# Three moves at the head of an attention-plus-MLP kernel: batch 0's sums inverted on ScalarE, batch 2 turned by DMA with its squares on VectorE, batch 1's last quad prepared earlier

## The chip, the cores and the metric

The kernel runs on one core of a Trainium2 chip. The metric is the device time of one execution in microseconds (us), as the median of several; lower is better. The core's engines each run their instructions in order: TensorE (PE in the profile; its weight loads are PEld), VectorE (DVE), ScalarE (ACT), GpSimd (POOL) and the queue of SyncE (SP), which here issues DMA transposes and output writes. SBUF and PSUM are memories of the core; in this kernel TensorE writes its results to PSUM. The span is the length of the one execution that was profiled.

## The reference

The inputs are q, k, v of shape (8 batches, 12 heads, 448 positions, 64) in float32 and two weights, 768x2048 and 2048x768.

```python
q_n = q / (norm(q, axis=-1) + 1e-6); k_n = k / (norm(k, axis=-1) + 1e-6)
scores = q_n @ k_n.T / tau                 # tau = 0.1
attn = softmax(scores)                     # the row sum divides
x = (attn @ v), heads side by side         # (3584, 768)
h = x @ w_in;  g = max(0.01 * h, h);  out = g @ w_out
```

## The kernel before

Each batch has six head pairs with two halves, so twelve *visits*. At a visit TensorE makes the scores of one half, ScalarE their exponentials. One visit later come parts of `weigh`: the row sums and the weighted values of a *quad* (four heads, two pairs). Layers 1 and 2 of the MLP for earlier tokens fill TensorE's time between visits. Meanwhile the q and k of the next batch are prepared: squares, their sums (`reduce`), the root (ScalarE), the inverse (VectorE), the multiply (`apply`), and the turn (transpose) so that the head dimension lies on partitions.

```python
def turn(b, what):                           # whole tensor, by DMA; batches 3 to 7
    xn, xt = st[what + "n", b], turned(b, what)
    nc.sync.dma_start_transpose(out=xt[...], in_=xn[...])

def turn_pair(b, p, eng=None):               # one pair, by TensorE; batches 0 to 2
    ...                                      # 8 transposes into a PSUM tile "mm"
    for i, what in enumerate("qk"):
        nc.vector.tensor_copy(out=turned(b, what)[...], in_=tp[:, i]...)

def inverse(b, g, sm, c0=0, c1=S):
    st["rs", b, g] = wk.tile([128, S], F32, name="rs")
    nc.vector.reciprocal(st["rs", b, g][:, c0:c1], sm[:, c0:c1])
    ...
def weigh(b, g, s, c0=0, c1=S):
    if s == 0:
        inverse(b, g, sums(b, g, c0, c1), c0, c1)   # sums: PSUM tile "pv", 2 buffers
    x_write(b, g, s, values(b, g, s, None, c0, c1), c0, c1)   # values: also "pv"
```

The two `pv` buffers matter: `values(b, g, 1)` takes the buffer that the sums of the same quad held, so TensorE can't start it before the inversion has read them. What is prepared for batches 1 and 2 during batches 0 and 1 stands in `early(b, n)`, n being the visit; its part for b == 1 is in the diff below. The order of issue in the program is the order of execution on each engine. (In the profiles Lnnn is a line of the kernel shown, so the same statement has other numbers in other kernels.) From batch 2 on, a general schedule is used:

```python
def after_scores(b, n):
    if b < 2:
        return early(b, n)
    if b + 2 < B and n < 2:
        load(b + 2, "qk"[n])                 # issued by GpSimd
    ...
    if n == 2:
        load(b + 1, "v")
        norm_sums(b + 1, "q")                # squares and reduce, both VectorE
```

Of the kernel before, what the change touches and what calls it, by code (L numbers as in the profile page):

```python
# [10 lines left out]
ACTF = mybir.ActivationFunctionType  # L11
# [5 lines left out]
def kernel(  # L17
# [18 lines left out]
    nc = tc.nc  # L36
# [4 lines left out]
    PK = S // NT  # L41
# [39 lines left out]
    st = {}  # L81


    def load(b, what, g0=0, g1=G):
        src = {"q": q_r, "k": k_r, "v": v_r}[what]
        if (what, b) not in st:
            if what == "v":
                st[what, b] = vpool.tile([PK, H, NT, D], BF16, name="v_bf")
            else:
                st[what, b] = bfpool.tile([PK, H, NT, D], BF16, name="qk_bf")  # L90
        if g1 - g0 == G:
            nc.gpsimd.dma_start(out=st[what, b], in_=src[b])  # L92
            return
        for g in range(g0, g1):
            nc.gpsimd.dma_start(out=st[what, b][:, g::G], in_=src[b][:, g::G])
# [19 lines left out]
    def norm_squares(b, what, eng, g0=0, g1=G):  # L115
        if (what + "n", b) not in st:
            st[what + "n", b] = inp.tile([PK, G, 2, NT, 2, D], BF16, name=f"{what}_n")
            st[what + "i", b] = small.tile([PK, G, 4, NT], F32, name=f"{what}_ni")
        for g in range(g0, g1):
            x, sq = by_quad(st[what, b])[:, g], squares(b, what, g, g + 1)[:, 0]  # L120
            if eng is nc.scalar:
                nc.scalar.activation(sq, x, func=ACTF.Square)
            else:
                eng.tensor_mul(sq, x, x)  # L124

    def norm_reduce(b, what, g0=0, g1=G):
        nc.vector.tensor_reduce(  # L127
            st[what + "i", b][:, g0:g1].rearrange("p g a t -> p (g a) t"),
            squares(b, what, g0, g1).rearrange("p g a t d -> p (g a) t d"),
            axis=AX.X, op=ALU.add,  # L130
        )

    def norm_sums(b, what, g0=0, g1=G):
        norm_squares(b, what, nc.vector, g0, g1)
        norm_reduce(b, what, g0, g1)

    def norm_root(b, what, g0=0, g1=G):
        ni = st[what + "i", b][:, g0:g1]
        nc.scalar.activation(ni, ni, func=ACTF.Ln, bias=tiny[:PK])
        nc.scalar.activation(ni, ni, func=ACTF.Exp, scale=0.5)  # L140

    def norm_inverse(b, what, g0=0, g1=G):
        ni = st[what + "i", b][:, g0:g1]
        nc.vector.tensor_scalar_add(ni, ni, 1e-6)
        nc.vector.reciprocal(ni, ni)  # L145

    def norm_apply(b, what, eng, g0=0, g1=G):
        x, xn, ni = by_quad(st[what, b]), st[what + "n", b], st[what + "i", b]
        for g in range(g0, g1):
            for j in range(2):  # L150
                ni_j = ni[:, g, 2 * j : 2 * j + 2]
                eng.tensor_tensor(  # L152
                    out=xn[:, g, j].rearrange("p t h d -> p h t d"),
                    in0=x[:, g, 2 * j : 2 * j + 2],
                    in1=ni_j.unsqueeze(3).to_broadcast([PK, 2, NT, D]),
                    op=ALU.mult,
                )


    def turned(b, what):  # L160
        if (what + "T", b) not in st:
            xt = tpool.tile([128, NT * HP * PK + 16], BF16, name=f"{what}T")
            nc.gpsimd.memset(xt[:, NT * HP * PK :], 0.0)
            st[what + "T", b] = xt
        return st[what + "T", b]

    def turn(b, what):
        xn, xt = st[what + "n", b], turned(b, what)
        nc.sync.dma_start_transpose(
            out=xt[:, : NT * HP * PK].rearrange("p (c n) -> p c n", n=PK),  # L170
            in_=xn.rearrange("p g j t h d -> p (g j t h d)"),
        )
# [21 lines left out]
    def scores(b, p, half, hold=False):  # L194

        qT, kT = st["qT", b], st["kT", b]
        if half == 0:
            st["pe", b, p] = epool.tile([PK, NT, 2, S], BF16, name="pe")
        wide = 128 if b > 2 else PK
        for i in range(2):  # L200
            ki = 2 * half + i
            sc = psc.tile([128, 2, 512], F32, name="sc")
            o = p * S + ki * PK
            for a in range(2):
                r = slice(64 * a, 64 * a + 64)
                nc.tensor.matmul(  # L206
                    out=sc[:wide, a, :S], lhsT=kT[r, o : o + wide],
                    rhs=qT[r, p * S : (p + 1) * S], start=True, stop=True,
                )
            st["exp", i] = (st["pe", b, p][:, ki], sc[:PK, :, :S])  # L210
            if i == 0 or not hold:
                exponential(i)
# [19 lines left out]
    def exponential(i):  # L232
        pe, sc = st["exp", i]
        nc.scalar.activation(out=pe, in_=sc, func=ACTF.Exp, scale=inv_tau)  # L234
# [10 lines left out]
    def x_place(b):  # L245


        if b % 2 == 0:
            st["x", b] = xpool.tile([128, KT, 512], BF16, name="xT")
            st["x64", b] = cpool.tile([128, KT, 64], BF16, name="x64")  # L250
        else:
            st["x", b] = xpool.tile([128, KT, 512], BF16, name="xT")
            nc.gpsimd.tensor_copy(out=st["x", b][:, :, 0:64], in_=st["x64", b - 1])

    def sums(b, g, c0=0, c1=S):
        sm = ppv.tile([128, S], F32, name="pv")
        columns(sm, b, g, lambda a, ki: ones[:PK, :], c0, c1)
        return sm

    def inverse(b, g, sm, c0=0, c1=S):  # L260
        st["rs", b, g] = wk.tile([128, S], F32, name="rs")
        nc.vector.reciprocal(st["rs", b, g][:, c0:c1], sm[:, c0:c1])  # L262
        if ("x", b) not in st:
            x_place(b)

# [96 lines left out]
    V, P, A = nc.vector, nc.gpsimd, nc.scalar  # L362
# [45 lines left out]
    sm = sums(0, 0, *one)  # L408
# [22 lines left out]
    sm = sums(0, 1, *one)  # L431
# [9 lines left out]
    sm = sums(0, 2, *one)  # L441
# [11 lines left out]
    def step(b, what, g0, g1, *steps):  # L453

        for name, eng in steps:
            if name == "squares":
                norm_squares(b, what, eng, g0, g1)
            elif name == "reduce":
                norm_reduce(b, what, g0, g1)
            elif name == "root":  # L460
                norm_root(b, what, g0, g1)
            else:
                norm_inverse(b, what, g0, g1)
                norm_apply(b, what, eng, g0, g1)

    def early(b, n):
        def both(to, g0, g1, name, eq=None, ek=None):
            step(to, "q", g0, g1, (name, eq))
            step(to, "k", g0, g1, (name, ek))

        if b == 0:
            if n == 0:
                both(1, 0, 1, "squares", P, P)
            elif n == 2:
                both(1, 0, 1, "reduce")
            elif n == 3:
                both(1, 1, 2, "squares", P, P)
            elif n == 4:
                both(1, 0, 1, "root")
            elif n == 5:  # L480
                both(1, 0, 1, "apply", V, P)
            elif n == 6:
                both(1, 1, 2, "reduce")
            elif n == 8:
                both(1, 1, 2, "root")
                both(1, 2, 3, "squares", P, P)
                load(2, "q")
            elif n == 9:
                both(1, 1, 2, "apply", V, P)
                load(2, "k")  # L490
            elif n == 11:
                both(1, 2, 3, "reduce")
        elif n == 1:
            both(1, 2, 3, "root")
            load(2, "v")
        elif n == 2:
            both(1, 2, 3, "apply", V, P)
        elif n == 4:
            step(2, "q", 0, 3, ("squares", P))
            load(3, "q")  # L500
        elif n == 5:
            step(2, "k", 0, 3, ("squares", P))
            load(3, "k")
        elif n == 6:
            step(2, "q", 0, 3, ("reduce", V))
        elif n == 7:
            step(2, "k", 0, 3, ("reduce", V))
            step(2, "q", 0, 3, ("root", A))
        elif n == 8:
            step(2, "q", 0, 3, ("apply", P))  # L510
            step(2, "k", 0, 3, ("root", A))
        elif n == 9:
            step(2, "k", 0, 3, ("apply", V))

    def after_scores(b, n):
        if b < 2:
# [22 lines left out]
            turn(b + 1, "k")  # L539

    turns = {
        (0, 7): (1, 0), (0, 8): (1, 1), (0, 10): (1, 2), (0, 11): (1, 3), (1, 3): (1, 4, 5),
        (1, 10): (2, 0, 1), (1, 11): (2, 2, 3), (2, 1): (2, 4, 5),
    }

    def after_dense(b, n):
# [15 lines left out]
    for b in range(B):  # L562
        for p in range(HP):
            for half in range(2):
                n = 2 * p + half
# [56 lines left out]
```

## Time and profile before

| | before |
|---|---|
| median | 481.35 us (479.99 to 481.79, 3 runs) |
| profiled span | 479.3 us |
| PE busy | 435.0 us, 91% |
| first scores of batch 2 (timeline of PE) | 107.52 us |
| longest wait of PE after the start | 4.66 us, until 102.20 |

The head of the profile page of the kernel before: busy time of each engine, then PE's busy tenths and its granted clock in 40 slices of 12 us.

```profile
PE 435.0 (91%) x3618; PEld 221.4 (46%) x3632; DVE 220.8 (46%) x267; ACT 269.3 (56%) x445; POOL 137.6 (29%) x152
...
PE   0788888758899999989899999998999999999996
...
PEclk9999999988999999998999999999999999999999
```

From slice 12 on, counted from 0 (144 us), PE is busy nearly all the time. What can be won lies before. The next lines are from the timeline of PE of the kernel before: start in us, duration in us, engine, source line, operation, output and inputs with shapes, count, and in brackets the idle time just ahead and what ended it.

```profile
96.95 0.59 PE L206 MATMUL sc<-qT,kT 64*112 64x448 bf16 x4
102.20 4.27 PE L319 MATMUL mm<-w_out_sb,hT 128*128 128x384 bf16 x16 [4.66 <-DVE kT L188]
...
107.52 0.59 PE L206 MATMUL sc<-qT,kT 64*112 64x448 bf16 x4
...
112.04 1.67 PE L239 MATMUL pv<-pe,v_bf 112*32 112x448 bf16 x16 [1.79 <-DVE rs L262]
```

At 102.20 PE had waited 4.66 us for the VectorE copy of kT: layer 2 needs a PSUM buffer that the turn of batch 2 holds until it is copied out. The timeline of VectorE of the kernel before shows why the copy was late:

```profile
88.14 2.95 DVE L262 RECIPROCAL rs<-pv 128x448 f32<-128x448 f32 x1
...
94.16 7.38 DVE L152 TENSOR_TENSOR k_n<-qk_bf,k_ni 112x512 bf16<-112x512 bf16 x6
101.47 0.38 DVE L188 COPY qT<-mm 128x448 bf16<-128x448 bf16 x1
```

Six multiplies of batch 2's k (94.16, 7.38 us) stood ahead of it. The same six operations, on GpSimd for q, ran at the same time. In windows of 2 us (busy time of PE, PEld, DVE, ACT, POOL with counts, then granted clock, DMA share, GB/s), the clock after the hole in the kernel before:

```profile
102.00:104.00 2.00, 1.80 (x6) 0.89 (x7) 0.74 (x3) 0.00 (x0) 0.77 (x1) 0.50 0.78 74
104.00:106.00 2.00, 2.00 (x10) 1.02 (x9) 0.00 (x0) 0.00 (x0) 0.00 (x0) 0.68 1.44 194
```

Granted clock 0.50 and 0.68: after the idle time TensorE ran at half speed, and the group of sixteen layer-2 matmuls took 4.27 us where others of the same kind took 2.77. The Trainium skill ("TensorE: Matmul & The Clock Gate", Part 1: The HAM clock gate) says that an idle window of about 3.4 us brings the array's clock to half. This hole agrees: 4.66 us idle, then clock 0.50.

### The profile page before, as it was taken

Reading aid. Unit: us, or ns where it says so; the run is one execution under the profiler, and the core shown is the slowest. Engines: PE = TensorE matmul, PEld = TensorE weight load, DVE = VectorE, ACT = ScalarE, POOL = GpSimd, SP = SyncE. Lnnn points to the kernel's source line nnn. Section 1 sums busy time; section 2 is a strip of 40 time slices with the busy share of each in tenths; the row PEclk is TensorE's granted clock in tenths of the full one; section 3 lists DMA queues with packets and bytes.
Section 4 is the critical chain, followed back from the end, with each engine's and each line's share of the span. In section 5 each row is a group of like instructions: output and inputs, shape, how many; then the busy total and the mean of one; then the engine's idle time right before and its main releaser. Section 6 shows DMA issues by size and latency. Waiting matters only on the chain.

```text
span 479.3 us, 8521 instructions
## 1 busy us (share of the span) xinstructions
PE 435.0 (91%) x3618; PEld 221.4 (46%) x3632; DVE 220.8 (46%) x267; ACT 269.3 (56%) x445; POOL 137.6 (29%) x152
## 2 busy tenths in 40 slices
PE   0788888758899999989899999998999999999996
PEld 0456644534344554544344554544434555454463
DVE  5976867865923087205923087208712312311000
ACT  3767567824675557653674557665774567543411
POOL 7555649450074012900073012700180000000000
PEclk9999999988999999998999999999999999999999
DMA  9999995557019860392419660455034110020022
GB/s 123 210 203 204 145 172 100 77 75 111 21 28 134 144 104 15 61 192 69 68 35 132 147 105 4 59 116 97 2 59 90 55 47 1 18 66 18 0 67 66
DMA packets 73924, 41.23 MB, mean 86 GB/s; under 512 B 29600, under 2 KB 73120, under 8 KB 73888
## 3 DMA queue, kind: packets, MB, share of 16 engines
q0 software_dynamic: 37728, 22.81, 34.5%
q1 hardware_dynamic: 36160, 17.90, 16.4%
q8 instruction: 28, 0.46, 0.4%
q14 instruction: 8, 0.07, 0.0%
HBM read 45.61 MB, written 11.01 MB: 118 GB/s over the span
## 4 chain that ended last, share of the span: by engine, by line
PE 76%; DVE 14%; DMA 3%; POOL 3%; ACT 2%; issue 1%; SPq 0%; POOLq 0%; ACTq 0%; DVEq 0%
PE mm L319 29%; PE mm L306 27%; PE pv L239 11%; PE sc L206 7%; DVE rs L262 3%; DVE k_ni L127 2%; DMA kT<-k_n 2%; DVE k_n L152 2%; DVE q_ni L127 2%; DVE q_n L152 2%; ACT pe L234 1%; POOL k_n L124 1%; POOL q_n L124 1%; PE sc L224 1%; PE mm L180 1%; DMA qk_bf<-in_q_dram 1%
## 5 line engine op out<-in xcount | busy, mean ns | idle before, releaser
L234 ACT ACTIVATE pe<-sc 112x896 bf16<-112x896 f32 (+2 forms) x192 | 167.9, 917 | 15.9 <-PE sc L224 10.2
L319 PE MATMUL mm<-w_out_sb,hT 128*128 128x384 bf16 x896 | 156.9, 332 | 4.7 <-DVE kT L188 4.7
L306 PE MATMUL mm<-xT,w_in_sb 128*128 128x512 bf16 (+3 forms) x850 | 155.1, 332 | 3.0 <-ACT hT L311 1.7
L262 DVE RECIPROCAL rs<-pv 128x448 f32<-128x448 f32 (+2 forms) x27 | 71.3, 2642 | 149.2 <-PE pv L239 149.2
L319 PEld LDWEIGHTS <-hT 128*128 128x128 bf16 x896 | 85.8, 99 | 74.7 <-issue 17.5
L306 PEld LDWEIGHTS <-w_in_sb 128*128 128x128 bf16 x864 | 76.5, 98 | 76.5 <-issue 18.1
L311 ACT ACTIVATE hT<-mm 128x512 bf16<-128x512 f32 (+3 forms) x144 | 71.8, 502 | 61.8 <-PE mm L306 61.2
L325 ACT COPY osb<-mm 128x384 f32<-128x384 f32 x56 | 26.8, 478 | 117.1 <-PE mm L319 84.3
L152 POOL TENSOR_TENSOR q_n<-qk_bf,q_ni 112x512 bf16<-112x512 bf16 x36 | 38.1, 1088 | 91.1 <-DVE q_ni L145 71.2
L206 PE MATMUL sc<-qT,kT 64*128 64x448 bf16 (+1 forms) x336 | 49.9, 360 | 8.2 <-ACT pe L234 6.0
L239 PE MATMUL pv<-pe,v_bf 112*32 112x448 bf16 (+2 forms) x864 | 48.1, 345 | 6.8 <-DVE rs L262 6.8
L152 POOL TENSOR_TENSOR k_n<-qk_bf,k_ni 112x512 bf16<-112x512 bf16 x40 | 41.8, 1071 | 7.8 <-DVE k_ni L145 4.7
L92 POOL DMA_DIRECT2D v_bf<-in_v_dram x8 | 7.5, 944 | 103.8 <-PE pv L239 103.7
L239 PEld LDWEIGHTS <-v_bf 112*32 112x32 bf16 x864 | 21.3, 99 | 26.4 <-issue 15.7
L206 PEld LDWEIGHTS <-kT 64*128 64x128 bf16 (+1 forms) x336 | 13.0, 103 | 38.5 <-issue 35.0
L127 DVE TENSOR_REDUCE k_ni<-k_n 112x16 f32<-112x1024 bf16 (+1 forms) x12 | 27.4, 2281 | 1.4 <-POOL k_n L124 1.2
L127 DVE TENSOR_REDUCE q_ni<-q_n 112x16 f32<-112x1024 bf16 (+1 forms) x12 | 27.3, 2277 | 0.2
L239 PE MATMUL pv<-pe,ones 112*32 112x448 bf16 (+2 forms) x432 | 24.5, 343 | 0.8 <-ACT pe L234 0.8
L278 DVE TENSOR_TENSOR xT<-pv,rs 128x448 bf16<-128x448 f32 x24 | 14.9, 622 | 20.4 <-PE pv L239 19.2
L281 DVE TENSOR_TENSOR xT<-pv,rs 128x384 bf16<-128x384 f32 (+2 forms) x30 | 14.3, 477 | 21.1 <-PE pv L239 19.5
L180 PE MATMUL mm<-ident,q_n 112*128 112x112 bf16 x72 | 7.7, 241 | 11.1 <-DVE q_n L152 10.5
L239 PEld LDWEIGHTS <-ones 112*32 112x32 bf16 x432 | 9.2, 97 | 13.1 <-issue 9.1
(48 smaller groups left out, 180.6 us busy)
## 6 DMA issues: line engine op xcount, KB each, us to landing
v_bf<-in_v_dram POOLq DMA_DIRECT2D x8, 672.0 KB, 7.5
qk_bf<-in_q_dram POOLq DMA_DIRECT2D x6, 672.0 KB, 7.4
qk_bf<-in_k_dram POOLq DMA_DIRECT2D x6, 672.0 KB, 9.4
w_in_sb<-in_moe_w_in_dram POOLq DMA_DIRECT2D x4, 768.0 KB, 19.1
w_out_sb<-in_moe_w_out_dram POOLq DMA_DIRECT2D x2, 1536.0 KB, 27.0
out_dram<-osb SPq DMA_DIRECT2D x16, 168.0 KB, 2.4
out_dram<-osb SPq DMA_DIRECT2D x16, 144.0 KB, 2.1
out_dram<-osb SPq DMA_DIRECT2D x16, 120.0 KB, 2.0
```

What stands on the lines that cost most here:

```text
L127: nc.vector.tensor_reduce(st[what + "i", b][:, g0:g1].rearrange("p g a t -> p (g a) t"), squares(b, what, g0, g1).rearrange("p g a t d -> ...
L152: eng.tensor_tensor(out=xn[:, g, j].rearrange("p t h d -> p h t d"), in0=x[:, g, 2 * j : 2 * j + 2], in1=ni_j.unsqueeze(3).to_broadcast([P ...
L206: nc.tensor.matmul(out=sc[:wide, a, :S], lhsT=kT[r, o : o + wide], rhs=qT[r, p * S : (p + 1) * S], start=True, stop=True,)
L234: nc.scalar.activation(out=pe, in_=sc, func=ACTF.Exp, scale=inv_tau)
L239: nc.tensor.matmul(out=dst[32 * a : 32 * a + 32, c0:c1], lhsT=weights(a, ki), rhs=st["pe", b, 2 * g + a // 2][:, ki, a % 2, c0:c1], start= ...
L262: nc.vector.reciprocal(st["rs", b, g][:, c0:c1], sm[:, c0:c1])
L278: nc.vector.tensor_mul(x[:, kt, 64:512], po, rs)
L281: nc.vector.tensor_mul(x[:, kt, c0:c], po[:, c0:c], rs[:, c0:c])
L306: nc.tensor.matmul(out=pm[:, :n], lhsT=w_in_sb[:, kt, m * 128 : (m + 1) * 128], rhs=st["x", b][:, kt, x0 : x0 + n], start=(kt == 0), stop= ...
L311: nc.scalar.activation(out=st["h", c][:, m, :n], in_=pm[:, :n], func=ACTF.Prelu, alpha=0.01)
L319: nc.tensor.matmul(out=po[:, :NH], lhsT=st["h", c][:, m, j0 : j0 + 128], rhs=w_out_sb[:, m, n * NH : (n + 1) * NH], start=(m == 0), stop=( ...
L325: nc.scalar.copy(out=osb, in_=po[:, :NH])
```

## The change

The intent can be read from the parts: take the slow VectorE reciprocals out of batch 0; take batch 2's transposes and their copies off TensorE and VectorE by using the DMA turn that later batches use; start batch 2's preparation earlier, for which batch 1's last quad must leave the shared buffers earlier.

```diff
-        wide = 128 if b > 2 else PK
+        wide = 128 if b > 1 else PK
@@ def inverse
-        nc.vector.reciprocal(st["rs", b, g][:, c0:c1], sm[:, c0:c1])
+        rs = st["rs", b, g][:, c0:c1]
+        if b == 0:
+            nc.scalar.activation(rs, sm[:, c0:c1], func=ACTF.Ln)
+            nc.scalar.activation(rs, rs, func=ACTF.Exp, scale=-1.0)
+        else:
+            nc.vector.reciprocal(rs, sm[:, c0:c1])
@@ def early, b == 1 (V, P, A: VectorE, GpSimd, ScalarE)
-        elif n == 1:
+        elif n == 0:
             both(1, 2, 3, "root")
             load(2, "v")
+        elif n == 1:
+            both(1, 2, 3, "apply", V, P)
+            load(3, "q")
         elif n == 2:
-            both(1, 2, 3, "apply", V, P)
-        elif n == 4:
-            step(2, "q", 0, 3, ("squares", P))
-            load(3, "q")
+            load(3, "k")
+        elif n == 3:
+            norm_sums(2, "q")
         elif n == 5:
-            step(2, "k", 0, 3, ("squares", P))
-            load(3, "k")
+            norm_sums(2, "k")
         elif n == 6:
-            step(2, "q", 0, 3, ("reduce", V))
+            step(2, "q", 0, 3, ("root", A), ("apply", P))
         elif n == 7:
-            step(2, "k", 0, 3, ("reduce", V))
-            step(2, "q", 0, 3, ("root", A))
-        elif n == 8:
-            step(2, "q", 0, 3, ("apply", P))
-            step(2, "k", 0, 3, ("root", A))
+            step(2, "k", 0, 3, ("root", A), ("apply", V))
         elif n == 9:
-            step(2, "k", 0, 3, ("apply", V))
+            turn(2, "k")
+            turn(2, "q")
@@ turns by TensorE
-        (0, 7): (1, 0), ..., (1, 3): (1, 4, 5),
-        (1, 10): (2, 0, 1), (1, 11): (2, 2, 3), (2, 1): (2, 4, 5),
+        (0, 7): (1, 0), ..., (1, 2): (1, 4, 5),
```

More of the change, by code (lines that the diff above doesn't have):

```diff
@@ L541 @@
     turns = {
-        (0, 7): (1, 0), (0, 8): (1, 1), (0, 10): (1, 2), (0, 11): (1, 3), (1, 3): (1, 4, 5),
-        (1, 10): (2, 0, 1), (1, 11): (2, 2, 3), (2, 1): (2, 4, 5),
+        (0, 7): (1, 0), (0, 8): (1, 1), (0, 10): (1, 2), (0, 11): (1, 3), (1, 2): (1, 4, 5),
     }
```

## The prediction

> **What bounds the kernel now.** TensorE: the page has PE busy 435.0 of 479.3 us (91%), the chain of waits is 76% PE. From 140 us on PE is near full (39.9 of 40 us between 340 and 420); only the first 132 us has anything to win. By the timeline of PE its waits there are: the start (12 us); in batch 0 the row-sum reciprocals (0.70 and 1.43 us of waiting in the first half, 1.35 at 65.0); in batch 1 one hole of 4.66 us (97.5 to 102.2), released by the VectorE copy of kT. That copy sits behind six VectorE multiplies of batch 2's k (94.16, 7.38 us; mean 1.23 beside GpSimd's multiplies against 0.65 alone). After the hole the granted clock is 0.50 and 0.68 for 4 us (windows of 2 us), and a 16-matmul group took 4.27 us against 2.77. The Trainium skill ("TensorE: Matmul & The Clock Gate", Part 1) says PE is throttled after an idle window of about 3.4 us; this hole agrees.
>
> **What the change does.**
> 1. Batch 0's six reciprocals (1.75 us for 256 columns, 1.35 for 192; 9.4 us of VectorE) become Ln and Exp on ScalarE, about 0.38 us each (estimate from the 128x256 Prelu, 0.38). PSUM is free after the Ln. Saved waits: 1 to 1.6 us by 36 us, 1.35 at 65. Part is lost at 59: the k multiplies on GpSimd wait for squares whose load ends at 53.2 anyway. Left: about 2 us.
> 2. Batch 2's six turn pairs leave PE: 0.95 us per two pairs and small gaps, 3 us in all, and 12 VectorE copies (3.6 us). They become two DMA transposes (3.2 to 8.2 us each in later batches).
> 3. Its squares go from GpSimd (11.3 us) to VectorE (3.6 us). The 4.66 us hole, as it stands, goes.
>
> **What it costs.** VectorE runs in order. norm_sums of q (5.2 us) now comes just before batch 1's first row-sum reciprocal, which should end near 79 instead of 77.9 us: about what was won so far is lost. Then ScalarE's root for k waits for the second reduce (near 86) and holds back activations: 1 to 2.5 us. Then the k multiply, 7.4 us beside GpSimd (the skill's "GPSIMD Engine Reference", section 1, says the two share SBUF interfaces; 1.23 against 0.65 agrees), stands before the second quad's reciprocal, at about 87 to 94. So I expect a new PE wait of 4 to 7 us at batch 1's tenth visit (values, near 91 to 97), again with a slow clock. The hole moves; it doesn't vanish. Turns end near 100 (k) and 104 (q), close to batch 2's first scores (before: 107.5); a wait there would be short.
>
> Sum: first scores of batch 2 about 1 to 3 us earlier, then 1.2 us from the removed last turns and 0.5 us from the full-width k weights; the PE-bound rest carries this shift to the end.
>
> **Prediction:** 477.5 us, 8 in 10 between 471 and 482. Faster by over 2%: 0.10; within 2%: 0.87; slower by over 2%: 0.03.
>
> **Right if** the profile shows: no PE wait for a kT copy near 100; a PE wait of several us on the batch-1 reciprocal behind the k multiplies, with low clock after it; PE's transposes 96 instead of 144; VectorE's row-sum reciprocals 21; PE from 140 on unchanged but shifted 2 to 5 us.
>
> **Wrong if** VectorE's k multiply runs near 0.65 us, so that the second hole is absent (then 8 to 10 us are won); if ScalarE, with the inversions in its queue, delays batch 0's exponentials and PE with them; or if the DMA turns land after batch 2's first scores are due.

## The result, and the profile after

The changed kernel takes 488.61 us (median of 4 runs, 488.38 to 489.77) against 481.09 (4 runs, 479.99 to 481.79): slower by 1.6%, ratio 1.0163 with a 95% interval of 1.0137 to 1.0189. Here and below a ratio is the mean time of one kernel's fast runs over that of the other's fast runs of the same rounds, so it isn't quite the ratio of the medians quoted.

| | before | after |
|---|---|---|
| profiled span | 479.3 | 487.8 us |
| PE busy | 435.0 | 435.2 us |
| first scores of batch 1 | 61.02 | 62.97 us |
| first scores of batch 2 | 107.52 | 116.62 us |
| from there to the end | 371.8 | 371.2 us |

The last two rows are sums of the rows above (span less the first scores). Batch 1's stretch grew from 46.50 to 53.65 us, by 7.15, while the start took 1.95 more and the rest 0.6 less; together that is the 8.5 us of the spans. (About 1.5 of the 1.95 us is a spell of slow clock from 50.8 to 54.2, which two other runs of the same instructions up to there did not have: see "Batch 0" below.) The page of the changed kernel, as before:

```profile
PE 435.2 (89%) x3570; PEld 219.6 (45%) x3584; DVE 214.7 (44%) x255; ACT 273.0 (56%) x457; POOL 127.1 (26%) x146
...
PE   0789887564899999997899999999899999999996
...
PEclk9999899967899999998999999999999999999999
```

Slices are 12.2 us here. Slices 7 to 9, counted from 0 (85 to 122 us), have fallen to 5, 6 and 4 tenths of PE. The timeline of PE of the changed kernel there:

```profile
92.17 0.59 PE L206 MATMUL sc<-qT,kT 64*112 64x448 bf16 x4
101.54 1.68 PE L239 MATMUL pv<-pe,v_bf 112*32 112x448 bf16 x16 [8.79 <-DVE rs L267]
103.16 2.10 PE L311 MATMUL mm<-xT,w_in_sb 128*128 128x128 bf16 x18
...
108.15 2.77 PE L324 MATMUL mm<-w_out_sb,hT 128*128 128x384 bf16 x16
116.62 0.93 PE L206 MATMUL sc<-qT,kT 64*128 64x448 bf16 x4 [5.70 <-DMA qT<-q_n]
...
122.23 1.69 PE L239 MATMUL pv<-pe,v_bf 112*32 112x448 bf16 x16 [0.71 <-DVE rs L267]
```

Where the kernel before waited once, the changed one waits twice: 8.79 us for the reciprocal, 5.70 us for the DMA turn of q. The first can be read on the timeline of VectorE of the changed kernel:

```profile
89.67 0.45 DVE L145 RECIPROCAL k_ni<-k_ni 112x48 f32<-112x48 f32 x1
90.16 8.47 DVE L152 TENSOR_TENSOR k_n<-qk_bf,k_ni 112x512 bf16<-112x512 bf16 x6
98.55 2.94 DVE L267 RECIPROCAL rs<-pv 128x448 f32<-128x448 f32 x1
```

The six k multiplies (now 8.47 us, 1.41 each) moved from visit 9 to visit 7, ahead of the second quad's reciprocal. By PE's timeline its sums were done at 89.04; it started at 98.55. For the second wait, first the timeline of GpSimd in the changed kernel:

```profile
89.79 8.29 POOL L152 TENSOR_TENSOR q_n<-qk_bf,q_ni 112x512 bf16<-112x512 bf16 x6 [16.62 <-PE pv L239]
...
98.37 0.98 POOL L92 DMA_DIRECT2D qk_bf<-in_q_dram  x1 [0.21 <-POOL kT L163]
99.35 0.94 POOL L92 DMA_DIRECT2D qk_bf<-in_k_dram  x1
```

and the timeline of SyncE's queue in the changed kernel:

```profile
98.78 7.08 SPq L169 DMA_TRANSPOSE kT<-k_n  x1
105.97 8.44 SPq L169 DMA_TRANSPOSE qT<-q_n  x1
```

The k turn is issued at 98.78, just after the k multiply. Almost at the same time (98.37 and 99.35) GpSimd issues the loads of batch 4's q and k: they belong to visits 0 and 1 of batch 2, but GpSimd has nothing else ahead of them and needs only the buffers of batch 2's q and k, which the multiplies have just freed. The transposes take 7.08 and 8.44 us, and PE starts 2.2 us after the second has ended (114.41). A turn of a later batch in the same run, without such company, takes 3.98 (149.05). The clock in windows of 2 us, changed kernel:

```profile
98.00:100.00 2.00, 0.00 (x0) 0.00 (x0) 2.00 (x2) 0.00 (x0) 1.79 (x5) 0.50 0.00 0
...
112.00:114.00 2.00, 0.00 (x0) 0.00 (x0) 0.00 (x0) 0.00 (x0) 0.00 (x0) 1.00 1.30 214
...
116.00:118.00 2.00, 1.38 (x12) 0.46 (x16) 0.00 (x0) 0.79 (x1) 0.00 (x0) 0.50 0.21 63
...
126.00:128.00 2.00, 2.00 (x14) 0.86 (x12) 1.97 (x2) 0.37 (x1) 0.00 (x0) 1.00 1.07 102
```

Besides the spell in batch 0, the clock is at half speed twice here: from 95 to 105 and from 116 to 126. An estimate of the cost, from group times at full and at half clock: the groups at 101.54 and 103.16 take 1.68 and 2.10 us against 0.94 and 1.37 in the kernel before, 1.5 us; the six groups from 116.62 to 123.84 lose another 4.0 against the same kinds later on. In the kernel before, three groups (4.27 for 2.77, 1.67 for 0.94, 3.68 for 2.77) lost 3.1.

### The profile page after: what moved, and what is told of

The parts are those of the page before. It is cut to its first block, busy times and chain, and to the rows that moved or that the text cites. A ratio compares the mean times of both kernels' runs of the same rounds, so it can differ in the third digit from the quotient of the medians.

```text
span 487.8 us, 8428 instructions
## 1 busy us (share of the span) xinstructions
PE 435.2 (89%) x3570; PEld 219.6 (45%) x3584; DVE 214.7 (44%) x255; ACT 273.0 (56%) x457; POOL 127.1 (26%) x146
## 4 chain that ended last, share of the span: by engine, by line
PE 75%; DMA 11%; DVE 7%; ACT 3%; SPq 2%; issue 1%; POOL 1%; POOLq 0%; ACTq 0%
PE mm L311 28%; PE mm L324 28%; PE pv L239 11%; PE sc L206 7%; DMA w_in_sb<-in_moe_w_in_dram 5%; DMA kT<-k_n 2%; DMA qT<-q_n 2%; DVE k_n L152 2%; ACT pe L234 2%; DMA qk_bf<-in_q_dram 1%; SPq L169 1%; DVE rs L267 1%; DVE q_n L152 1%; ACT hT L316 1%; DVE k_ni L127 1%
## 5 line engine op out<-in xcount | busy, mean ns | idle before, releaser
L324 PE MATMUL mm<-w_out_sb,hT 128*128 128x384 bf16 x896 | 154.3, 328 | 0.0
L267 DVE RECIPROCAL rs<-pv 128x448 f32<-128x448 f32 x21 | 62.1, 2955 | 157.4 <-PE pv L239 157.4
L311 PEld LDWEIGHTS <-w_in_sb 128*128 128x128 bf16 x864 | 77.6, 99 | 78.4 <-issue 19.8
L239 PE MATMUL pv<-pe,v_bf 112*32 112x448 bf16 (+2 forms) x864 | 50.0, 355 | 11.1 <-DVE rs L267 10.9
L239 PE MATMUL pv<-pe,ones 112*32 112x448 bf16 (+2 forms) x432 | 26.3, 364 | 1.1 <-ACT pe L234 1.1
L180 PE MATMUL mm<-ident,q_n 112*128 112x112 bf16 x48 | 5.6, 254 | 10.8 <-DVE q_n L152 10.5
```

Of the source, the lines that this page charges most:

```text
L239: nc.tensor.matmul(out=dst[32 * a : 32 * a + 32, c0:c1], lhsT=weights(a, ki), rhs=st["pe", b, 2 * g + a // 2][:, ki, a % 2, c0:c1], start= ...
L267: nc.vector.reciprocal(rs, sm[:, c0:c1])
L311: nc.tensor.matmul(out=pm[:, :n], lhsT=w_in_sb[:, kt, m * 128 : (m + 1) * 128], rhs=st["x", b][:, kt, x0 : x0 + n], start=(kt == 0), stop= ...
L324: nc.tensor.matmul(out=po[:, :NH], lhsT=st["h", c][:, m, j0 : j0 + 128], rhs=w_out_sb[:, m, n * NH : (n + 1) * NH], start=(m == 0), stop=( ...
```

## The experiments

The medians of the kernel before were 482.88, 481.63, 481.03 and 482.07 us on chips 8, 14, 2 and 14, so medians are compared only roughly; the ratios are safer. All kernels gave correct results.

### Late loads

The loads of batch 4 are put behind a load that has to wait, so that none runs during the two turns. Diff against the changed kernel:

```diff
-        if b + 2 < B and n < 2:
+        if b > 2 and b + 2 < B and n < 2:
             load(b + 2, "qk"[n])
@@
             load(b + 1, "v")
+            if b == 2:
+                load(4, "q")
+                load(4, "k")
```

> The changed kernel with batch 4's q and k loads issued behind batch 3's v load (which waits for a values group), so that no load runs during batch 2's two DMA transposes. Theory A (the transposes end late because the loads of batch 4 share the DMA with them): each transpose takes 3.2 to 4.5 us instead of 7.1 and 8.4, the 5.7 us wait of TensorE at batch 2's first scores shrinks to 0 to 1, the slow clock after it goes, and the time falls by 6 to 10 us to 479 to 483 us; the 8.8 us wait at the reciprocal stays. Rival B (transposes of this batch are slow in themselves, or only the late k multiply counts): time within 2 us of 488.6.

Measured: 482.33 us (4 runs), ratio to before 1.0025 (0.9974 to 1.0076), so 6.3 us below the changed kernel's median. The timeline of GpSimd with late loads:

```profile
115.56 0.98 POOL L92 DMA_DIRECT2D v_bf<-in_v_dram  x1 [18.93 <-PE pv L239]
116.53 0.94 POOL L92 DMA_DIRECT2D qk_bf<-in_q_dram  x1
```

and of SyncE's queue:

```profile
97.25 3.28 SPq L169 DMA_TRANSPOSE kT<-k_n  x1
100.64 3.38 SPq L169 DMA_TRANSPOSE qT<-q_n  x1
```

The transposes fell from 7.08 and 8.44 us to 3.28 and 3.38, and the wait of PE at batch 2's first scores (at 109.27) vanished, while the wait of 8.78 us for the reciprocal stayed. Theory A holds for the second wait: the turns were slow because of the loads beside them. (Not all slow clock after it went: PE waited 1.82 us for a reciprocal at 113.75, with a clock of 0.50 after.) The Trainium skill ("Trainium Kernel Development and Optimization", Key Constraints) says that DMAs of the Sync, Scalar and GpSimd queues all run on the same 16 engines and interleave. That agrees: 3.28 us alone, 7.08 in company.

### The k multiply behind the reciprocal

```diff
-            step(2, "k", 0, 3, ("root", A), ("apply", V))
+            step(2, "k", 0, 3, ("root", A))
+        elif n == 8:
+            step(2, "k", 0, 3, ("apply", V))
```

> The changed kernel with batch 2's k multiply one visit later, so behind the second quad's reciprocal in VectorE's order. Theory A (two waits in a row; the DMA transposes, which start only when the k multiply ends, set when batch 2 can start): the 8.8 us wait falls to under 2 us, but the k multiply ends 1 to 3 us later, the wait at batch 2's first scores grows from 5.7 to 11 to 16 us, time 487 to 491. Rival C (the reciprocal behind the k multiply is what costs): time falls by 6 to 9 us.

Measured: 485.64 us, ratio 1.0092 (1.0037 to 1.0146): about 3 us below the changed kernel, in neither theory's range. PE's timeline had no wait for the reciprocal over 1.5 us in batch 1, and one of 13.89 us for the q turn, as theory A said. The line of PE in this run:

```profile
112.80 0.93 PE L206 MATMUL sc<-qT,kT 64*128 64x448 bf16 x4 [13.89 <-DMA qT<-q_n]
```

What the theory had wrong is seen on VectorE's timeline:

```profile
87.48 2.90 DVE L267 RECIPROCAL rs<-pv 128x448 f32<-128x448 f32 x1
...
91.72 5.63 DVE L152 TENSOR_TENSOR k_n<-qk_bf,k_ni 112x512 bf16<-112x512 bf16 x6
```

The multiply started 3.1 us later than in the run with late loads (91.72 against 88.63) and still ended at nearly the same time (97.35 against 97.09): it took 5.63 us instead of 8.46, and GpSimd's multiplies of q ran beside it only until 95.0, which would explain it. In this run GpSimd's load of batch 4's k waited for VectorE's k multiply by the timeline of GpSimd:

```profile
97.65 0.94 POOL L92 DMA_DIRECT2D qk_bf<-in_k_dram  x1 [1.37 <-DVE k_n L152]
```

So the multiplies do release the loads; the turns, beside loads here too, took 6.37 and 6.58 us. Letting the reciprocal go first was free. Rival C falls all the same: a hole of 8.8 us was taken away and only about 3 us came of it (the interval overlaps that of the changed kernel), since batch 2 can't start before its turns have landed.

### Both moves

> Both moves at once. Theory A: first wait under 2 us, transposes 3.2 to 4.5 us each, wait at batch 2's first scores 5 to 9 us; time about that of the late loads alone, within 3 us, 478 to 483. Rival C: adds 6 to 9 us of gain to whatever the late loads alone give, so 471 to 475.

Measured: 479.53 us, ratio 0.9957 (0.9909 to 1.0004). The edit is the two diffs above together. PE's one long wait with both moves:

```profile
107.57 0.93 PE L206 MATMUL sc<-qT,kT 64*128 64x448 bf16 x4 [7.43 <-DMA qT<-q_n]
```

2.8 us below the late loads alone, in theory A's range. The first hole was taken away and became a wait for the q turn (7.43 us), in a chain of multiply, k turn, q turn. The loss of the changed kernel is now accounted for by the order of two pieces of work and the time of two loads; the three moves as such, so repaired, come to about the time of before.

### Batch 0's inversions back on VectorE

```diff
-        if b == 0:
+        if b < 0:
             nc.scalar.activation(rs, sm[:, c0:c1], func=ACTF.Ln)
```

> The changed kernel with batch 0's inversions back on VectorE. Theory D (moving them to ScalarE gave nothing, because in batch 0 TensorE then waited for w_in's load and for GpSimd's k multiplies, and VectorE's earlier multiply collided with GpSimd's squares): time within 2 us of the changed kernel, first scores of batch 1 at 61 to 63 us. Rival E (the inversions on ScalarE gave the 2 us that the prediction counted): 2 us or more slower than the changed kernel.

Measured: 488.18 us, ratio 1.0143 (1.0092 to 1.0195), against 1.0163 for the changed kernel: the same. First scores of batch 1 at 61.00 us. The inversions were worth nothing in this kernel.

### Batch 2 turned by TensorE again

```diff
-        wide = 128 if b > 1 else PK
+        wide = 128 if b > 2 else PK
@@ early
-            turn(2, "k")
-            turn(2, "q")
+            pass
@@ turns
+        (1, 10): (2, 0, 1), (1, 11): (2, 2, 3), (2, 1): (2, 4, 5),
```

> The changed kernel with batch 2 turned by TensorE as before the change; its early squares and multiplies on VectorE and the inversions on ScalarE stay. Theory A (the DMA turns cost a 5.7 us wait plus slow clock and save 3 us of TensorE): no wait for a DMA at batch 2's first scores, 8.8 us hole at the reciprocal stays, 482 to 486 us. Rival: the turns by DMA were a gain in themselves and the k multiply alone is to blame: 489 to 492.

Measured: 484.22 us, ratio 1.0055 (1.0023 to 1.0086), 4.4 us below the changed kernel; the wait of 8.78 us at the reciprocal stayed and there was no DMA wait at batch 2's first scores. As built, the DMA turns cost more than they saved; what is left of the change is still slower than before.

### Batch 1's sums on ScalarE too

On top of the late loads:

```diff
-        if b == 0:
+        if b < 2:
             nc.scalar.activation(rs, sm[:, c0:c1], func=ACTF.Ln)
```

> The changed kernel with late loads and with batch 1's row sums inverted on ScalarE too, so that no reciprocal stands behind VectorE's norm sums or k multiply. Theory A: the 8.8 us and 1.45 us waits for the reciprocal go, ScalarE gains three inversions of about 1 us; TensorE then waits 3 to 6 us for the q turn at batch 2's first scores; 474 to 478 us. Rival F (ScalarE is too full in batch 1, so that the exponentials slip): waits of TensorE for exponentials grow by the same amount and the time stays at 480 to 483.

Measured: 475.87 us, ratio 0.9870 (0.9833 to 0.9907). No wait for a reciprocal of batch 1 remains; PE waits 5.75 us for the q turn at 107.31, and its waits for ScalarE have hardly grown (0.82 and 0.84 us for exponentials against 0.82 and 0.75 in the changed kernel, 1.22 against 0.84 for a layer-1 activation). Rival F falls: ScalarE had room.

### Batch 2 in quads

On top of the late loads. The k multiply and both turns are cut in three.

```diff
+    def turn_quad(b, what, g):
+        xn, xt, w = st[what + "n", b], turned(b, what), 2 * NT * PK
+        nc.sync.dma_start_transpose(
+            out=xt[:, g * w : (g + 1) * w].rearrange("p (c n) -> p c n", n=PK),
+            in_=xn[:, g].rearrange("p j t h d -> p (j t h d)"))
@@ early, b == 1
         elif n == 7:
-            step(2, "k", 0, 3, ("root", A), ("apply", V))
+            step(2, "k", 0, 3, ("root", A))
+            step(2, "k", 0, 1, ("apply", V))
+        elif n == 8:
+            turn_quad(2, "k", 0)
+            turn_quad(2, "q", 0)
+            step(2, "k", 1, 2, ("apply", V))
         elif n == 9:
-            turn(2, "k")
-            turn(2, "q")
+            turn_quad(2, "k", 1)
+            turn_quad(2, "q", 1)
+            step(2, "k", 2, 3, ("apply", V))
+        elif n == 10:
+            turn_quad(2, "k", 2)
+            turn_quad(2, "q", 2)
```

> The changed kernel with late loads, and batch 2's k multiply and both turns cut into three quads, with the second quad's reciprocal after the first third of the multiply. Theory A: the wait for the reciprocal falls from 8.8 to 2.5 to 4 us, the last turn lands no later than before, the wait at batch 2's first scores is under 2 us; 474 to 478 us. If small turns cost nearly as much each as a whole one (over 2 us), the last turn lands later and the time is 479 to 483.

Measured: 476.38 us, ratio 0.9891 (0.9860 to 0.9922). The wait for the reciprocal fell to 2.98 us and PE had no wait over 0.7 us for a turn. A third of a turn took 1.22 to 1.99 us.

### The kernel before, with its k multiply in quads

This starts from the kernel before: no part of the change is in it.

```diff
-            step(2, "k", 0, 3, ("apply", V))
+            step(2, "k", 0, 1, ("apply", V))
+        elif n == 11:
+            step(2, "k", 1, 2, ("apply", V))
@@ after_scores, b >= 2
+        if b == 2 and n == 0:
+            step(2, "k", 2, 3, ("apply", V))
```

> The kernel before with nothing changed but batch 2's k multiply cut into three quads, each ahead of the turn that needs it. Theory A (the 4.66 us hole of the kernel before was six multiplies standing ahead of four copies on VectorE, and its slow clock about 3 us more): hole under 1 us, time 3 to 7 us less than before: 474 to 478. If the hole only moves to the next turns: within 2 us of before.

Measured: 474.57 us, ratio 0.9854 (0.9827 to 0.9882). The timeline of PE of this kernel where the hole was:

```profile
98.55 0.59 PE L206 MATMUL sc<-qT,kT 64*112 64x448 bf16 x4
99.06 2.78 PE L319 MATMUL mm<-w_out_sb,hT 128*128 128x384 bf16 x16
```

and of VectorE:

```profile
95.54 2.65 DVE L152 TENSOR_TENSOR k_n<-qk_bf,k_ni 112x512 bf16<-112x512 bf16 x2
98.22 0.39 DVE L188 COPY qT<-mm 128x448 bf16<-128x448 bf16 x1
```

The copies follow the first two multiplies, the hole and its slow clock are gone (layer 2 at 99.06 takes 2.78 us), and 7 us with them. This is the wait at which the change aimed; a reordering of VectorE alone removes it.

### The inversions alone, and combinations

`inv_only` is the kernel before with batch 0's inversions on ScalarE. `split_act01` and `split_act1` are the kernel before with the k multiply in quads and the sums of batches 0 and 1, or of batch 1 only, on ScalarE. `act01_quads` is the changed kernel with late loads, the sums of batches 0 and 1 on ScalarE and batch 2 in quads: all repairs together. All edits are those above; the condition in `inverse` is the only new one:

```diff
 inv_only:               if b == 0:
 split_act01, act01_quads: if b < 2:
 split_act1:             if b == 1:
```

> The kernel before with nothing changed but batch 0's inversions on ScalarE. Theory D (they gain nothing at batch 1's first scores, for there other things set the pace: w_in's load, and GpSimd's k multiplies, which wait for VectorE): first scores of batch 1 at 61 to 63 us, the wait of 1.35 us at 65 gone, time within 2 us of before. Rival E (the prediction's 2 us): 2 to 4 us faster than before.

> The kernel before with batch 2's k multiply in quads (turns still on TensorE) and the row sums of batches 0 and 1 inverted on ScalarE. The waits for the reciprocal at 92.7 and 107.4 us (0.71 and 1.79) go: 2 to 3 us less than the split alone, 470 to 473 us.

> As the one before, with only batch 1's row sums on ScalarE and batch 0's on VectorE. If batch 0's inversions gain nothing by being on ScalarE (theory D), the time is within 2 us of the one before; if they gain the prediction's 2 us, it is 2 us or more slower.

> The changed kernel with late loads, batch 1's row sums on ScalarE too and batch 2's k multiply and turns in quads: both of the waits that the change brought are repaired. Theory A: no wait over 2 us of TensorE between 60 and 130 us, 469 to 473 us. If the turns of the last quad or ScalarE now hold TensorE back: 473 to 477.

| kernel | median of 6 runs | ratio to before (95% interval) |
|---|---|---|
| inv_only | 479.79 us | 0.9979 (0.9937 to 1.0020) |
| split_act01 | 469.46 us | 0.9766 (0.9720 to 0.9811) |
| split_act1 | 471.17 us | 0.9803 (0.9760 to 0.9846) |
| act01_quads | 466.07 us | 0.9691 (0.9649 to 0.9733) |

`inv_only` came out as theory D expected: first scores of batch 1 at 61.94 us, no wait of 1.35 us at 65, time within 2 us. `split_act01` came out just below its range, 4 us below the split alone by ratio where 2 to 3 were expected. `split_act1` is within 2 us of it (1.7), as theory D expected. `act01_quads` is the best version found, 3.1% faster than before and about 22 us faster than the changed kernel (medians). It also came out below its expected range. Its timeline of PE:

```profile
91.15 0.94 PE L246 MATMUL pv<-pe,v_bf 112*32 112x448 bf16 x16
...
99.02 0.55 PE L213 MATMUL sc<-qT,kT 64*128 64x448 bf16 x4
```

of ScalarE:

```profile
88.49 0.56 ACT L271 ACTIVATE rs<-pv 128x448 f32<-128x448 f32 x1
89.08 0.58 ACT L272 ACTIVATE rs<-rs 128x448 f32<-128x448 f32 x1
```

and of SyncE's queue:

```profile
98.94 1.25 SPq L169 DMA_TRANSPOSE qT<-q_n  x1
```

The values group at 91.15 follows its scores with no wait, and batch 2's first scores come at 99.02 instead of 107.52 or 116.62, with the last turn still on its way: they need only the first quad. The inversion took 0.56 + 0.58 us on ScalarE; the reciprocal takes 2.95 on VectorE. With both kinds of turn freed of their waits, the DMA version is 3.4 us faster than the TensorE version (466.07 against 469.46). The two kernels differ in more than the turn, though: batch 2's squares are on VectorE in one and on GpSimd in the other, and its preparation starts earlier in the first. So the change as a whole pays once repaired; what the DMA turn alone is worth was not measured.

### What two parts are worth by themselves

`quad_only` is the kernel before with only batch 1's last quad one visit earlier (root at visit 0, apply at 1, turn at 2). `act1_quads` is `act01_quads` with batch 0's inversions on VectorE.

```diff
 quad_only, early, b == 1
-        elif n == 1:
+        elif n == 0:
             both(1, 2, 3, "root")
             load(2, "v")
-        elif n == 2:
+        elif n == 1:
             both(1, 2, 3, "apply", V, P)
@@ turns
-        (1, 3): (1, 4, 5)
+        (1, 2): (1, 4, 5)
 act1_quads, inverse
-        if b < 2:
+        if b == 1:
```

> The kernel before with nothing changed but batch 1's last quad prepared and turned one visit earlier. Theory (it only clears the way for batch 2's early squares, nothing waits for it): the 4.66 us hole stays and the time is within 2 us of before. Rival: an earlier turn holds TensorE back or frees it, over 2 us either way.

> The repaired kernel (late loads, batch 1's row sums on ScalarE, batch 2 in quads) with batch 0's inversions back on VectorE. If they are worth the prediction's 2 us or more on ScalarE: 468 to 470 us; theory D: 465 to 467.5 us, within 1.5 us of the repaired kernel.

Measured: `quad_only` 481.54 us, ratio 1.0003 (0.9961 to 1.0046), with a hole of 4.67 us as before: no gain or loss of its own. `act1_quads` 470.04 us (five runs), ratio 0.9744 (0.9714 to 0.9774). One of its six executions, the profiled one, took 728.86 us with a mean granted clock of 0.574; it is left out as slow. The other five lie above theory D's range (465 to 467.5) and at the end of the other (468 to 470), so theory D failed here. Compared by ratio with `act01_quads`, the inversions on ScalarE are worth about 0.0053 of 481 us, 2.5 us; in the pair (`split_act1` against `split_act01`) 1.7 us; alone 1.2 us, within the noise. So theory D is right for the changed kernel and not in general: they gain little or nothing while the VectorE chain of batch 1 sets the pace afterwards, and roughly the predicted 2 us once the large waits are gone. The intervals are too wide to settle the size closer than about 2 us.

## Why the prediction was wrong

- **The time.** It said 477.5 us, 471 to 482; measured 488.61. The class it thought likeliest, within 2%, came true only by luck, for the sign was wrong: it expected a gain of 4 us and there was a loss of 7.5.
- **The hole that moves: right in place, too small in size.** It named the wait at batch 1's tenth visit, the k multiplies ahead of the second quad's reciprocal, with a slow clock after it. Predicted 4 to 7 us, measured 8.79. It had the multiplies start at about 87 and take 7.4 us; they started at 90.16, since the VectorE chain before them ran later than reckoned, and took 8.47, with GpSimd beside them all the time.
- **The step that failed: "a wait there would be short" at batch 2's first scores.** The wait was 5.70 us, and a second slow-clock stretch followed, which the prediction hadn't at all. It had read that later batches' turns take 3.2 to 8.2 us and put the end of the q turn near 104; it was 114.4, with PE starting at 116.62. Among its own reasons to be wrong it named turns that land late, but it gave them no time. It didn't ask what GpSimd would issue at that moment, though the record had a hint: the slowest of those turns in the kernel before, 8.25 us at 205.44, follows two loads that GpSimd issued at 201.31 and 202.28. The multiplies that free the turns' inputs also free the buffers of batch 4's loads, so loads and turns start together by construction. `loads_late` shows it: 3.28 and 3.38 us, and 6.3 us of time.
- **Batch 0: "about 2 us left" were not there.** The waits for the reciprocals went (0.70, 1.43 and 1.35 us in the kernel before), but PE then waited elsewhere: 1.33 us for w_in's load at 33.5, and 1.72 us for GpSimd's k multiply at 50.78, against 0.68 before. That multiply starts at 49.68, no earlier than in the kernel before (49.11): PE only came to it sooner and waited longer. In this profile VectorE's q multiply of the first quad ran beside GpSimd's squares and took 2.65 us (46.51) where it took 1.29 (47.30) in the kernel before. But this collision, which theory D names, is not what PE's wait needs: with late loads, the same instructions up to there, the q multiply took 1.29 us, GpSimd's k multiply started at 48.99, and PE still waited 1.71. By the traces GpSimd waits there for VectorE's inverse of k in all three; what holds that back was not tested. In the changed kernel's profile the clock was at 0.50 for 3.4 us after this wait, about 1.5 us by the group times; with late loads it was not, and batch 1's first scores came at 61.44 instead of 62.97. By experiment the part is worth nothing in the changed kernel and up to 2.5 us in the repaired one.

The lines for that are, from the timeline of VectorE of the kernel before,

```profile
47.30 1.29 DVE L152 TENSOR_TENSOR q_n<-qk_bf,q_ni 112x512 bf16<-112x512 bf16 x2
```

of VectorE of the changed kernel,

```profile
46.51 2.65 DVE L152 TENSOR_TENSOR q_n<-qk_bf,q_ni 112x512 bf16<-112x512 bf16 x2
```

and of PE of the changed kernel:

```profile
33.54 1.03 PE L311 MATMUL mm<-xT,w_in_sb 128*128 128x256 bf16 x8 [1.33 <-DMA w_in_sb<-in_moe_w_in_dram]
...
50.78 0.55 PE L180 MATMUL mm<-ident,k_n 112*128 112x112 bf16 x4 [1.72 <-POOL k_n L152]
```

From the timeline of VectorE with late loads,

```profile
47.18 1.29 DVE L152 TENSOR_TENSOR q_n<-qk_bf,q_ni 112x512 bf16<-112x512 bf16 x2
```

and of PE with late loads:

```profile
50.09 0.37 PE L180 MATMUL mm<-ident,k_n 112*128 112x112 bf16 x4 [1.71 <-POOL k_n L152]
```

- **Right:** no wait for a kT copy near 100; 96 transposes on PE; 21 reciprocals of row sums on VectorE; the rest of the kernel unchanged (371.8 and 371.2 us), though shifted 9.1 us later where 2 to 5 us earlier was expected. The fear that ScalarE would be too full did not come true.

As a check of the sum, from the first scores of batch 1 to the third visit's scores of batch 2 (118.37 and 127.53 us) the stretch grew by 7.2 us. An estimate from the profiles: the waits over 1 us in it rose from 8.9 (1.35, 1.06, 4.66, 1.79) to 15.9 us (1.45, 8.79, 5.70), the slow clock's cost from 3.1 to 5.5, and about 3 us of turns left PE: 6.4 in all. The slow clock in it is that of these two executions only: in the profile of `inv_undone` the spell at batch 2's first scores lasted 6.83 us instead of 10.24.

## What to carry to other kernels

Before moving a long block of work earlier on an in-order engine, list what then stands behind it, and cut the block so that short urgent instructions pass: here six multiplies had to be three pairs. When an engine finishes earlier, ask which transfers its freed buffers release, and whether they run beside a transfer that something waits for. Two waits in a row hide each other: taking away either alone gave about 3 and 6 us, both 9, and only cutting the blocks and moving the inversions as well gave the 22.

## What the Trainium skill lacked or had wrong

- "GPSIMD Engine Reference" (section 1) says that VectorE and GpSimd contend for SBUF with two-input instructions, but gives no size there. Here a 112x512 bf16 multiply took 0.65 us on VectorE alone and 1.23 to 1.41 beside GpSimd's, which rose from 1.03 to about 1.38 (8.29 for six). So twelve of them in parallel on both took 8.47 us; by an estimate from these numbers VectorE alone would need 7.8.
- "DMA: Bandwidth & Descriptors" gives a bandwidth for DMA transposes but no figure for one beside other transfers: one turn of 112x3072 bf16 took 3.28 us alone and 6.37 to 8.44 beside two loads; one of a third of that size 1.22 to 1.99.
- "TensorE: Matmul & The Clock Gate" (Part 1) says that the full clock comes after at least one busy window of about 3.4 us. Here it could take much longer: matmuls resumed at 116.62 in the changed kernel and the clock was full at 125.9; in `inv_undone`, with nearly the same waits, they resumed at 116.21 and it was full at 121.5. Worked out from the granted clock in windows of 0.5 us, taken as either 0.50 or 1.00, the slow spells of the fast profiles lasted 3.41, 6.83, 10.24 or 13.65 us, so whole steps of 3.41. And a wait well under the page's idle window of about 3.4 us could be enough to lose it: 1.72 us at 50.78 (changed) and 1.79 us at 112.04 (before), though not in every execution.
- No page that I read names Ln followed by Exp with scale -1 as a reciprocal on ScalarE. It took 0.56 + 0.58 us for 128x448 against 2.95 on VectorE, and all runs with it were correct. "ScalarE: Activation LUTs" (What it computes) warns off ScalarE's own Reciprocal and sends the reader to VectorE's.
- No page explains one execution of 728.86 us at a mean granted clock of 0.574 on a single core. In its profile the clock is 0.53 to 0.56 from 30 to 700 us (windows of 10 to 200 us), with PE busy 77 to 100% of each.
